# Attention on one core: both 64 by 64 corners side by side ahead of the value product, and the stores of x and of squared keys issued by GpSimd

## The chip, the core and the metric

The kernel runs on one core of one Trainium2 chip. The core has TensorE (PE, matmuls), VectorE (DVE), ScalarE (ACT), GpSimd (POOL) and SyncE (SP); each runs its own instructions in the order in which they were issued, and they wait for one another by semaphores. DMAs are issued from the engines' queues: in the kernel before nearly all by SyncE. The metric is the device time of one execution in microseconds (us), as the median of several runs. Less is better.

## What is computed

Four batches of 448 tokens, 12 heads of 64 columns (768 in all). Attention with a sigmoid in the place of the softmax, then a gated layer with squared keys, then a Fourier mix, a normalisation and two more matmuls:

```python
scores = scale * np.matmul(q, k.transpose(0, 1, 3, 2)) - np.log(S)
attn = 1.0 / (1.0 + np.exp(-scores))
x = np.matmul(attn, v)                      # heads side by side: B, S, 768
xk = mu_k * x + (1.0 - mu_k) * x_prev       # x_prev: one token earlier
xr = mu_r * x + (1.0 - mu_r) * x_prev
k = np.maximum(xk @ w_k, 0.0)
v = k * k @ w_v
y = v / (1.0 + np.exp(-(xr @ w_r)))
mixed = np.real(np.fft.fft(np.fft.fft(y, axis=1), axis=2))
u = y + mixed
un = (u - mean(u)) / np.sqrt(var(u) + 1e-06)
out = u + np.maximum(un @ w_ch1, 0.0) @ w_ch2
```

All in float32. Where it pays, the kernel splits a matrix into a high and a low part (names with `h` and `l`) and takes three matmuls of the fast kind instead of one in full float32.

## The kernel before

The program is written by a planner. Its class `Order` keeps a planned time of its own; generators for heads, keys, loads and weights are woken at due times and issue instructions when they are woken, with modelled costs. What comes out is one fixed order of instructions on each engine; on the chip nothing is reordered, only waited for.

The change lies in the attention stage, roughly the first 220 us. Two heads of one batch share 128 partitions and are a pair of columns; there are 24 such head pairs, `pairs`, numbered `i` from 0 to 23, six to a batch, and called heads below. The loop in `attention` takes two of them at a time. The 448 tokens of a head are three blocks of 128 and a rest of 64, the corner. For heads i and i + 1, from i = 6 on, a period goes like this:

- `begin(i - 2)` and `attnv` (twice): the value product of the two heads before. `begin` multiplies the two corners of the sigmoid (`sg_c`) with 64 rows of `v`, in 64x64 tiles of the array; `attnv` adds the six full blocks of each head (`sg`), in 128x64 tiles. Both sum into PSUM tiles `av`.
- `both(i)`: first `corner(i)`, the 64x64 scores of both heads (`sc_c`) in full float32 from raw `q` and `k`, then `scores(i)`, six score tiles `sc` of head i in 64x128 tiles, a stretch of key matmuls, `scores(i + 1)`, and a longer stretch of key matmuls.
- After each score tile ScalarE makes its sigmoid (`weigh`).
- `join` copies a finished `av` out of PSUM into `x` (ScalarE), stores `x` in DRAM, mixes it with the row of tokens before (`mix_k`) and splits it into `xkh` and `xkl`.
- `keys` multiplies them with the key weights, 18 matmuls for a tile `k`. The matmuls wait in a list (`feed`) and are issued one by one between the other steps. `key_done` takes a finished tile: ReLU out of PSUM and square (both `kt`), a cast to the high half of `kp` (ScalarE), the low half (VectorE), and the store of both halves, 448 KB, in DRAM. Its name there is `k2_d`; the views print `k_d<-kp`.

Buffers set what waits. Scores, corners, and the products `av` of heads 6 and on share six PSUM slots (`ps2`) in turn; key tiles have banks of their own (`bank`). `kp`, `kt` and `x` have two buffers each, so the cast into the third `kp` waits until the store of the first has landed, and `x` is overwritten when its store has landed. The raw `q` and `k` of two heads are loaded (960 KB in all) when `corner` of the two before has read theirs; `divide` then makes their halves `qh`, `ql`, `kh`, `kl`. In the gaps VectorE also splits weights (`wr_raw` to `wrh`, `wrl`, and `first_raw` to `first`); GpSimd clears a column of each `x` and stores the split `first` weights in DRAM, and does no more.

Heads 2 and 4 (`TURNS`) are an earlier form of the loop, in which the second `attnv` runs inside `both`.

Of the kernel before, what the change touches and what calls it, by code (L numbers as in the profile page):

```python
# [12 lines left out]
F32 = mybir.dt.float32  # L13
# [25 lines left out]
TURNS = (2, 4)  # L39
# [241 lines left out]
def build(tc, ap):  # L281
    nc = tc.nc
    V, G = nc.vector, nc.gpsimd
    o = Order(nc)
# [70 lines left out]
    x_d = [[dram.tile([128, S + 1], F32, name=f"x_d{b}_{p}") for p in range(NP)] for b in range(B)]  # L355
    k2_d = [[dram.tile([128, 2, S], F32, name=f"k2_d{b}_{f}") for f in range(NF)] for b in range(B)]
# [36 lines left out]
    pairs = [(b, p) for b in range(B) for p in range(NP)]  # L393
# [54 lines left out]
    def weigh(i, n, ps):  # L448
        sg = att.tile([128, S], F32, tag="sg", name=f"sg_{i}_{n}", bufs=2 * len(places) + 3)
        o.at["sg", i, n] = o.act(sg, ps[:, 0:S], AF.Sigmoid, bias=bias_s, scale=1.0 / math.sqrt(DH))  # L450
        sg_t[i, n] = sg

    def slot(name):
        return ps2.tile([128, 512], F32, tag="sc", name=name)
# [3 lines left out]
    def scores(i):  # L458
        k, q = pair_t["k", i], pair_t["q", i]
        for c in range(3):  # L460
            ps = [slot(f"sc_{i}_{2 * c + j}") for j in range(2)]
            if i < WHOLE:
                for j in range(2):
                    o.mm(ps[j][:, 0:S], k[half[j], c], q[half[j]], True, True, 0.39)
            else:
                for t, (a, b) in enumerate(TERMS):
                    for j in range(2):
                        o.mm(ps[j][:, 0:S], k[a][half[j], c], q[b][half[j]], t == 0, t == 2, 0.107)
            if c == 0:
                yield from o.others()  # L470
            for j in range(2):
                weigh(i, 2 * c + j, ps[j])
            yield from o.others()

    def corner(i):
        yield from o.need(*(("raw", w, i + m) for m in range(2) for w in "kq"))
        ps = [slot(f"sc_{i}_c{j}") for j in range(2)]
        for j in range(2):
            for m in range(2):
                k, q = raw_t["k", i + m], raw_t["q", i + m]  # L480
                o.mm(ps[j][half[m], 0:S], k[half[j], 3, 64 * j : 64 * j + 64], q[half[j]], True, True, 0.21)
        o.at["corner", i] = o.now
        yield from o.others()
        for j in range(2):
            weigh(i, f"c{j}", ps[j])
        yield from o.others()

    def soon(*keys):
        o.quiet = all(k in o.at for k in keys)

    def both(i, t0, turn=None):
        if i > 0:
            yield from corner(i)
        yield from o.need(("k", i), ("q", i))
        yield from scores(i)
        if i == 0:
            yield from corner(i)
        o.at["pair", i] = o.now
        o.quiet = o.quiet and i < WHOLE
        if turn:  # L500
            yield from turn
        if i >= WHOLE:
            yield t0 + (PACES[0] - AHEAD) * (len(o.feed) > 0)
            soon(("k", i + 1), ("q", i + 1))
            yield t0 + PACES[0] * (len(o.feed) > 0)
        yield from o.need(("k", i + 1), ("q", i + 1))
        yield from scores(i + 1)
        o.at["pair", i + 1] = o.now
        o.quiet = False

    def begin(i):
        ps = [(bank if i < WHOLE else slot)(f"av_{i + m}") for m in range(2)]
        yield from o.need(("sg", i, "c0"), ("sg", i, "c1"))
        for m in range(2):
            v = pair_t["v", i + m]
            for j in range(2):
                o.mm(ps[m][half[j], 0:S], v[half[m], 3, j], sg_t[i, f"c{j}"][half[m]], True, False, 0.21, skip=True)
        yield from o.others()
        av_t[i], av_t[i + 1] = ps

    def attnv(i):
        v = pair_t["v", i]
        for n, (c, j) in enumerate(places):
            yield from o.need(("sg", i, n))
            sg = sg_t.pop((i, n))
            o.mm(av_t[i][half[j], 0:S], v[:, c, j], sg, False, c == 2, 0.39, skip=True)
            if i % 2 and n == 2 and i < len(pairs) - 2 and i + 1 not in TURNS:
                g = i + 1
                soon(*(("raw", w, g + m) for w in "kq" for m in range(2)), ("k", g), ("q", g))
            yield from o.others()  # L530
        o.at["av", i] = o.now
        o.spawn(join(i, av_t.pop(i)), o.now + 0.2)
        yield from o.others()

    def join(i, ps):
        if i > 1:
            yield from o.issued(("mixed", i - 2))
        x = att.tile([128, S + 1], F32, tag="x", name=f"x_{i}")
        G.memset(x[:, 0:1], 0.0)
        yield o.act(x[:, 1 : S + 1], ps[:, 0:S])  # L540
        b, p = pairs[i]
        o.dma(x_d[b][p], x)
        if b > 1:
            yield from o.issued(("key", b - 2))
        xh = mop.tile([128, S], F32R, tag=f"xkh{p}", name=f"xkh_{i}")
        xl = mop.tile([128, S], F32R, tag=f"xkl{p}", name=f"xkl_{i}")
        xk_t[b, p] = (xh, xl)
        yield from mix(x, mu_k, att, p, f"k{i}", xh, xl, ("xk", b, p))
        o.at["mixed", i] = o.now

    def mix(x, mu, pl, p, nm, xh, xl, key, bufs=2):
        xk = pl.tile([128, S], F32, tag="mix", name=f"mix_{nm}", bufs=bufs)
        early = nm[0] == "k" and int(nm[1:]) < WHOLE
        if early:
            yield o.ts(xk, x[:, 1 : S + 1], mu[:, 0, p : p + 1], None, ALU.mult, ALU.bypass)
        else:
            yield from o.calm()
            yield o.act(xk, x[:, 1 : S + 1], AF.Copy, scale=mu[:, 0, p : p + 1])
        yield o.stt(xk, x[:, 0:S], mu[:, 1, p : p + 1], xk, ALU.mult, ALU.add)
        if early:  # L560
            V.tensor_copy(xh, xk)
            yield o.spend(V, 0.34)
        else:
            yield from o.calm()
            yield o.act(xh, xk)
        o.at[key] = t = o.sub(V, xl, xk, xh)
        yield t
# [6 lines left out]
    def attention():  # L574
        for i in range(0, len(pairs) + 2, 2):
            t0 = o.now
            turn = None
            if i > 0:
                yield from o.need(("v", i - 2), ("v", i - 1))
                yield from begin(i - 2)  # L580
                yield from attnv(i - 2)
                turn = attnv(i - 1)
                if i not in TURNS:
                    yield from turn
                    turn = None
            if i < len(pairs):
                yield from both(i, t0, turn)
            yield t0 + PACES[1] * (len(o.feed) > 0)
        yield from o.need(("xk", B - 1, NP - 1))
        o.at["attention"] = o.now  # L590

    def key_done(b, f, ps):
        t = mop.tile([128, S], F32, tag="kt", name=f"kt_{b}_{f}")
        o.act(t, ps, AF.Relu)
        yield from o.calm()
        yield o.act(t, t, AF.Square)
        parts = mop.tile([128, 2, S], F32R, tag="kp", name=f"kp_{b}_{f}")
        yield from o.calm()
        yield o.act(parts[:, 0], t)
        yield o.sub(V, parts[:, 1], t, parts[:, 0])  # L600
        o.at["k2_d", b, f] = o.dma(k2_d[b][f], parts.bitcast(F32)) + 2.0
        yield o.now

    def keys():
        for b in range(B):
            yield from o.issued(("av", NP * b + NP - 1))
            for f in range(NF):
                yield from o.need(("wk", f))

                def pair(t, b=b, f=f):  # L610
                    return wkh[:, f, t], wkl[:, f, t], *xk_t[b, t]

                ks = {p: ("xk", b, p) for p in range(NP)}
                yield from o.tile(partial(bank, f"k_{b}_{f}"), KD, pair, partial(key_done, b, f), None, ks)
                while len(o.feed) > 6:
                    yield o.now + 0.1
            while o.feed:
                yield o.now + 0.05
            o.at["key", b] = o.now
# [40 lines left out]
    for what in "kqv":  # L660
        o.spawn(prepare(what))
    o.spawn(attention())
    o.spawn(weights(), LATER)
    o.spawn(keys())
# [606 lines left out]
    for v, (g, ps) in enumerate(VISITS):  # L1271
        for j in range(2):
            i = 2 * (v - NG + PL) + j
# [469 lines left out]
```

## Time and profile before

| what | us |
|---|---|
| median of 3 runs | 1141.82 (1141.53 to 1143.3) |
| profiled execution, its own time | 1139.96 |
| span in the profile, first to last instruction | 1138.2 |
| TensorE busy | 1118.6 |
| VectorE busy | 810.6 |
| ScalarE busy | 649.2 |
| GpSimd busy | 16.1 |

The granted TensorE clock is 0.997 of full speed over the span. All rows come from the one profiled execution; its times are counted from the span's start. On the chain of work that ended last, 88% of the span is TensorE. Timelines show each instruction's start and length; instructions of an engine overlap a little, so the step from one to the next is read from their starts, or from a length less the overlap. One 64x64 matmul in the program is two rows on TensorE.

### The profile page before, as it was taken

Reading aid. Unit: us, or ns where it says so; the run is one execution under the profiler, and the core shown is the slowest. Engines: PE = TensorE matmul, PEld = TensorE weight load, DVE = VectorE, ACT = ScalarE, POOL = GpSimd, SP = SyncE. Lnnn points to the kernel's source line nnn. Section 1 sums busy time; section 2 is a strip of 40 time slices with the busy share of each in tenths; the row PEclk is TensorE's granted clock in tenths of the full one; section 3 lists DMA queues with packets and bytes.
Section 4 is the critical chain, followed back from the end, with each engine's and each line's share of the span. In section 5 each row is a group of like instructions: output and inputs, shape, how many; then the busy total and the mean of one; then the engine's idle time right before and its main releaser. Section 6 shows DMA issues by size and latency. Waiting matters only on the chain.

```text
span 1138.2 us, 16784 instructions
## 1 busy us (share of the span) xinstructions
PE 1118.6 (98%) x5908; PEld 975.0 (86%) x5908; DVE 810.6 (71%) x1306; ACT 649.2 (57%) x1165; POOL 16.1 (1%) x49
## 2 busy tenths in 40 slices
PE   9999999999999999989999999989999999999998
PEld 3476676799999989979999999879999999999997
DVE  3876767566624678799896565677657679976887
ACT  6788877766632333334686666667755444554442
POOL 0000001100000000000000000000000000000000
PEclk9999999999999999999999999999999999999999
DMA  7765789667939786536967988999887448945432
GB/s 247 237 231 202 241 325 342 256 231 262 335 136 313 278 305 226 179 134 227 298 230 249 301 300 276 319 318 360 271 332 267 135 151 283 360 145 184 160 99 86
DMA packets 116309, 279.65 MB, mean 246 GB/s; under 512 B 13248, under 2 KB 58496, under 8 KB 116096
## 3 DMA queue, kind: packets, MB, share of 16 engines
q1 hardware_dynamic: 113472, 266.29, 68.4%
q0 software_dynamic: 2464, 11.83, 2.8%
q8 instruction: 46, 0.75, 0.3%
q10 hardware_dynamic: 288, 0.46, 0.1%
q14 instruction: 39, 0.32, 0.1%
HBM read 184.80 MB, written 93.73 MB: 245 GB/s over the span
## 4 chain that ended last, share of the span: by engine, by line
PE 88%; DVE 5%; DMA 4%; ACT 2%; issue 1%; SPq 0%; DVEq 0%; ACTq 0%
PE m L213 23%; PE k L213 9%; PE f_Y L213 9%; PE v L213 8%; PE r L213 8%; PE av L213 6%; PE f_X L213 6%; PE f_W L213 6%; PE sc L213 5%; PE f L213 4%; PE pq L213 1%; PE sc_c L213 1%; DVE out L248 1%; PE pa L213 1%; PE qa L213 1%
## 5 line engine op out<-in xcount | busy, mean ns | idle before, releaser
L213 PE MATMUL m<-hs,sw 128*128 128x448 f32 x1512 | 303.7, 362 | 0.9 <-DVE hs L248 0.8
L213 PEld LDWEIGHTS m<-hs,sw 128*128 128x128 f32 x1512 | 283.3, 188 | 21.1 <-DVE hs L248 2.0
L265 ACT CAST sw<-w 128x768 fp32r<-128x768 f32 x84 | 70.0, 833 | 90.7 <-PE m L213 50.3
L265 ACT CAST hs<-r 128x896 fp32r<-128x896 f32 x84 | 78.9, 940 | 65.3 <-DVE r L248 65.3
L248 DVE TENSOR_TENSOR sw<-w,sw 128x768 fp32r<-128x768 f32 x84 | 80.2, 955 | 49.2 <-ACT sw L265 49.0
L213 PE MATMUL v<-k,wvh 128*128 128x448 f32 x384 | 111.5, 365 | 0.0
L248 DVE TENSOR_TENSOR hs<-r,hs 128x896 fp32r<-128x896 f32 x84 | 91.3, 1087 | 5.9 <-ACT hs L265 5.9
L267 ACT ACTIVATE sg<-sc,bias_s 128x448 f32<-128x448 f32 x144 | 78.3, 649 | 12.5 <-PE sc L213 12.4
L213 PE MATMUL f_Y<-T,blk 128*128 128x448 f32 x360 | 78.8, 367 | 4.3 <-ACT u L265 3.5
L213 PE MATMUL f_W<-T,blk 128*128 128x448 f32 x360 | 77.9, 364 | 0.4 <-DVE blk L248 0.4
L213 PEld LDWEIGHTS f_Y<-T,blk 128*128 128x128 f32 x360 | 68.1, 190 | 10.0 <-ACT u L265 4.2
L213 PEld LDWEIGHTS v<-k,wvh 128*128 128x128 f32 x384 | 71.9, 188 | 4.8 <-issue 0.4
L213 PEld LDWEIGHTS f_W<-T,blk 128*128 128x128 f32 x360 | 67.9, 189 | 5.4 <-DVE blk L248 0.8
L213 PE MATMUL k<-xkh,wkh 128*128 128x448 f32 x192 | 70.7, 368 | 0.9 <-ACT kt L267 0.9
L213 PE MATMUL k<-xkl,wkh 128*128 128x448 f32 x192 | 70.3, 366 | 0.0
L213 PE MATMUL v<-k,wvl 128*128 128x448 f32 x192 | 70.0, 365 | 0.0
L213 PE MATMUL k<-xkh,wkl 128*128 128x448 f32 x192 | 70.0, 364 | 0.0
L213 PE MATMUL f<-un,w1h 128*128 128x448 f32 x192 | 57.1, 374 | 4.5 <-DVE un L248 2.7
L267 ACT ACTIVATE w_raw<-w_raw 128x384 f32<-128x384 f32 x80 | 44.3, 553 | 23.9 <-DMA w_raw<-in_w 23.9
L213 PE MATMUL av<-sg,v 128*64 128x448 f32 x288 | 57.2, 544 | 0.0
L265 ACT CAST blk<-a 128x384 fp32r<-128x384 f32 x80 | 40.4, 513 | 28.3 <-PE f_Y L213 7.8
L256 DVE SCALAR_TENSOR_TENSOR w<-w_raw,w 128x384 uint32<-128x384 uint32 x60 | 33.3, 555 | 28.6 <-ACT w L267 24.6
(200 smaller groups left out, 2071.1 us busy)
## 6 DMA issues: line engine op xcount, KB each, us to landing
w<-v_d SPq DMA_DIRECT2D x84, 384.0 KB, 3.2
w_raw<-in_w SPq DMA_DIRECT2D x80, 384.0 KB, 4.6
r<-h_d SPq DMA_DIRECT2D x48, 448.0 KB, 5.8
k_d<-kp SPq DMA_DIRECT2D x32, 448.0 KB, 3.9
k<-k_d SPq DMA_DIRECT2D x32, 448.0 KB, 6.1
h_d<-h SPq DMA_DIRECT2D x56, 224.0 KB, 4.2
a<-w_d SPq DMA_DIRECT2D x32, 384.0 KB, 5.0
v_d<-w SPq DMA_DIRECT2D x48, 192.0 KB, 4.7
```

The lines of the kernel that those rows point to most:

```text
L213: self.nc.tensor.matmul(out, lhs, rhs, start=start, stop=stop, skip_group_check=skip)
L248: eng.tensor_tensor(out, a, c, op=op)
L256: self.nc.vector.scalar_tensor_tensor(out, a, scalar, c, op0=op0, op1=op1)
L265: self.nc.scalar.copy(out, a)
L267: self.nc.scalar.activation(out, a, fn, **kw)
```

## The change

`corner(i)` is called from `attention` ahead of `begin(i - 2)` for i = 6, 8, ... 22, and from `both` only for heads 2 and 4 (and 0, as before). The store of `x` (24 of 224.5 KB) and that of the squared keys (32 of 448 KB) get GpSimd as their engine (`G`).

```diff
     def both(i, t0, turn=None):
-        if i > 0:
+        if i in TURNS:
             yield from corner(i)
...
         yield o.act(x[:, 1 : S + 1], ps[:, 0:S])
         b, p = pairs[i]
-        o.dma(x_d[b][p], x)
+        o.dma(x_d[b][p], x, G)
...
             if i > 0:
+                if i < len(pairs) and i not in TURNS:
+                    yield from corner(i)
                 yield from o.need(("v", i - 2), ("v", i - 1))
                 yield from begin(i - 2)
                 yield from attnv(i - 2)
...
         yield o.sub(V, parts[:, 1], t, parts[:, 0])
-        o.at["k2_d", b, f] = o.dma(k2_d[b][f], parts.bitcast(F32)) + 2.0
+        o.at["k2_d", b, f] = o.dma(k2_d[b][f], parts.bitcast(F32), G) + 2.0
```

What a due time moves, the planner moves with it. Three places show it, all around heads 12 to 15; names carry running numbers, which differ between the two kernels. (In `kp_6` the 6 is the key tile within its batch.)

ScalarE from the high half of `kp_6` to the first sigmoid of head 14, before (`x` of heads 12 and 13, `sg_c` and `sg` of head 14):

```order
L265 CAST kp_6_1494<-kt_6_1428 128x448
L267 ACTIVATE kt_7_1505<-k_7_1426 128x448
L267 ACTIVATE kt_7_1505<-kt_7_1505 128x448
L265 CAST kh_1527<-k_1355 128x512
L265 CAST qh_1534<-q_1357 128x448
L265 CAST kp_7_1540<-kt_7_1505 128x448
L265 COPY x_1550<-av_1521 128x448
L265 COPY x_1582<-av_1522 128x448
L267 ACTIVATE sg_c_1585<-sc_c_1570,bias_s 128x448
L267 ACTIVATE sg_c_1587<-sc_c_1571,bias_s 128x448
L267 ACTIVATE sg_0_1602<-sc_0_1589,bias_s 128x448
```

and now:

```order
L265 CAST kp_5_1465<-kt_5_1407 128x448
L267 ACTIVATE kt_7_1512<-k_7_1434 128x448
L267 ACTIVATE kt_7_1512<-kt_7_1512 128x448
L265 CAST kp_6_1516<-kt_6_1437 128x448
L267 ACTIVATE sg_c_1542<-sc_c_1528,bias_s 128x448
L267 ACTIVATE sg_c_1544<-sc_c_1529,bias_s 128x448
L265 CAST kp_7_1559<-kt_7_1512 128x448
L265 COPY x_1570<-av_1546 128x448
L265 COPY x_1600<-av_1547 128x448
L267 ACTIVATE sg_0_1603<-sc_0_1589,bias_s 128x448
```

The corners' sigmoids come ahead of `kp_7` and of the two copies `x<-av` instead of behind them; the halves of `q` and `k` that stood here come earlier, ahead of `kp_5`.

VectorE from the low half of `kp_5` on, before (`wr_bits`, `wrh` and `wrl` are the split of a receptance weight):

```order
L248 TENSOR_TENSOR kp_5_1441<-kt_5_1397,kp_5_1441 128x448
L248 TENSOR_TENSOR xkl_1322<-mix_k_1323,xkh_1321 128x448
L256 SCALAR_TENSOR_TENSOR wr_bits<-wr_raw,wr_bits 128x768
L248 TENSOR_TENSOR kl_1476<-k_1336,kh_1475 128x512
L248 TENSOR_TENSOR ql_1481<-q_1338,qh_1480 128x448
L248 TENSOR_TENSOR kp_6_1494<-kt_6_1428,kp_6_1494 128x448
L256 SCALAR_TENSOR_TENSOR wr_bits<-wr_raw,wr_bits 128x768
L248 TENSOR_TENSOR kl_1528<-k_1355,kh_1527 128x512
L248 TENSOR_TENSOR ql_1535<-q_1357,qh_1534 128x448
L248 TENSOR_TENSOR kp_7_1540<-kt_7_1505,kp_7_1540 128x448
L344 CAST wrh_294<-wr_bits 128x768
L248 TENSOR_TENSOR wrl_295<-wr_bits,wrh_294 128x768
```

and now, from that weight's first bits:

```order
L256 SCALAR_TENSOR_TENSOR wr_bits<-wr_raw,wr_bits 128x768
L248 TENSOR_TENSOR ql_1481<-q_1314,qh_1480 128x448
L256 SCALAR_TENSOR_TENSOR wr_bits<-wr_raw,wr_bits 128x768
L248 TENSOR_TENSOR kl_1484<-k_1316,kh_1483 128x512
L248 TENSOR_TENSOR xkl_1389<-mix_k_1390,xkh_1388 128x448
L248 TENSOR_TENSOR xkl_1341<-mix_k_1342,xkh_1340 128x448
L344 CAST wrh_294<-wr_bits 128x768
L248 TENSOR_TENSOR wrl_295<-wr_bits,wrh_294 128x768
L248 TENSOR_TENSOR kp_5_1465<-kt_5_1407,kp_5_1465 128x448
L248 TENSOR_TENSOR kp_6_1516<-kt_6_1437,kp_6_1516 128x448
L248 TENSOR_TENSOR kp_7_1559<-kt_7_1512,kp_7_1559 128x448
```

All three `kp` now stand behind `wrh` and `wrl`; `kp_5` had been ahead of both steps on `wr_bits`.

TensorE from the last two value products of head 13 on, before:

```order
L213 MATMUL av_1522<-sg_4_1466,v_1311 64x448
L213 MATMUL av_1522<-sg_5_1468,v_1311 64x448
L213 MATMUL sc_c_1570<-q_1338,k_1336 64x448
L213 MATMUL sc_c_1570<-q_1357,k_1355 64x448
L213 MATMUL sc_c_1571<-q_1338,k_1336 64x448
L213 MATMUL sc_c_1571<-q_1357,k_1355 64x448
L213 MATMUL sc_0_1589<-qh_1480,kh_1475 128x448
```

and now, from the last key matmul ahead of the product:

```order
L213 MATMUL k_0_1510<-xkh_1111,wkl 128x448
L213 MATMUL sc_c_1528<-q_1299,k_1301 64x448
L213 MATMUL sc_c_1528<-q_1314,k_1316 64x448
L213 MATMUL sc_c_1529<-q_1299,k_1301 64x448
L213 MATMUL sc_c_1529<-q_1314,k_1316 64x448
L213 MATMUL av_1546<-sg_c_1304,v_1128 64x448
L213 MATMUL av_1546<-sg_c_1306,v_1128 64x448
L213 MATMUL av_1547<-sg_c_1304,v_1332 64x448
L213 MATMUL av_1547<-sg_c_1306,v_1332 64x448
L213 MATMUL av_1546<-sg_0_1359,v_1128 64x448
```

The four `sc_c` have moved from behind the 16 matmuls of the product to its start, directly ahead of the four `av<-sg_c`. The same holds for the other eight pairs; nothing else moves on TensorE.

On GpSimd the stores stand in one queue with the cleared columns: here first the column of `x` of head 12, then the stores of `kp_5`, of that `x`, of `kp_6` and of `kp_7`, the column of the next `x` and its store.

## Rows read from the trace of the kernel before

**Rows 1.** The page, its part 1: busy us (share) and instructions of each engine.

```profile
PE 1118.6 (98%) x5908; PEld 975.0 (86%) x5908; DVE 810.6 (71%) x1306; ACT 649.2 (57%) x1165; POOL 16.1 (1%) x49
```

**Rows 2.** Table by stretches: us, then busy us (instructions) by engine, clock, DMA share, GB/s.

```profile
100.00:160.00 60.00, 59.85 (x362) 40.38 (x361) 43.55 (x68) 47.89 (x93) 3.55 (x10) 1.00 0.72 257
```

**Rows 3.** Waits, 0 to 262: engine, line, waited for: us in total, times, longest us.

```profile
PE k L213 <- ACT kt L267: 0.9, 3, 0.5
PE warm L657 <- DVE bias_s L387: 0.9, 1, 0.9
...
ACT kp L265 <- DMA k_d<-kp: 3.1, 4, 1.3
```

**Rows 4.** Timeline of TensorE: start us, us, engine, line, op, out<-in, shape, count.

```profile
89.01 0.98 PE L213 MATMUL av<-sg_c,v 64*64 64x448 f32 x8
89.92 4.73 PE L213 MATMUL av<-sg,v 128*64 128x448 f32 x24
94.59 0.98 PE L213 MATMUL sc_c<-q,k 64*64 64x448 f32 x8
95.50 0.47 PE L213 MATMUL sc<-qh,kh 64*128 64x448 f32 x2
95.81 0.37 PE L213 MATMUL sc<-ql,kh 64*128 64x448 f32 x2
96.01 0.37 PE L213 MATMUL sc<-qh,kl 64*128 64x448 f32 x2
...
97.22 0.49 PE L213 MATMUL sc<-qh,kl 64*128 64x448 f32 x2
97.64 0.47 PE L213 MATMUL k<-xkl,wkh 128*128 128x448 f32 x1
```

**Rows 5.** Timeline of TensorE, a period and two periods later: the last two score tiles.

```profile
117.28 0.50 PE L213 MATMUL sc<-qh,kh 64*128 64x448 f32 x2
...
138.17 0.49 PE L213 MATMUL sc<-qh,kh 64*128 64x448 f32 x2
```

**Rows 6.** Timeline of ScalarE, heads 12 to 15; in brackets idle time ahead and its releaser.

```profile
106.75 0.59 ACT L265 CAST xkh<-mix_k 128x448 fp32r<-128x448 f32 x1
...
108.14 0.66 ACT L265 CAST kh<-k 128x512 fp32r<-128x512 f32 x1
108.67 0.59 ACT L265 CAST qh<-q 128x448 fp32r<-128x448 f32 x1
...
111.99 0.57 ACT L265 CAST kp<-kt 128x448 fp32r<-128x448 f32 x1 [0.23 <-DMA k_d<-kp]
112.96 0.53 ACT L265 COPY x<-av 128x448 f32<-128x448 f32 x1 [0.40 <-PE av L213]
...
126.75 0.60 ACT L265 CAST xkh<-mix_k 128x448 fp32r<-128x448 f32 x1
```

**Rows 7.** Timeline of VectorE in the same stretch.

```profile
109.88 0.95 DVE L256 SCALAR_TENSOR_TENSOR wr_bits<-wr_raw,wr_bits 128x768 uint32<-128x768 uint32 x1
110.75 0.69 DVE L248 TENSOR_TENSOR kl<-k,kh 128x512 fp32r<-128x512 f32 x1
...
114.43 0.62 DVE L248 TENSOR_TENSOR kp<-kt,kp 128x448 fp32r<-128x448 f32 x1
114.97 0.55 DVE L344 CAST wrh<-wr_bits 128x768 fp32r<-128x768 f32 x1
115.55 0.96 DVE L248 TENSOR_TENSOR wrl<-wr_bits,wrh 128x768 fp32r<-128x768 f32 x1
```

**Rows 8.** Stores: `k_d<-kp` by SyncE, 112 to 119; `w_d<-first_bits` by GpSimd, 138 to 206, 206 to 222.

```profile
DMA to landing us min/median/max: 4.1/5.8/7.5
...
L274 POOL DMA_DIRECT2D w_d<-first_bits x6: 544/547/829, 139.0 to 197.8; - x6
DMA to landing us min/median/max: 4.6/6.0/8.2
...
DMA to landing us min/median/max: 3.0/3.1/3.2
```

## The prediction

> **What bounds the kernel now.** I read the page first: TensorE is busy nearly all of the span, GpSimd 16 us of it [rows 1]. Then the table by stretches: of the 60 us from 100 to 160, in the attention stage, TensorE is busy 59.85, VectorE and ScalarE about 44 and 48 [rows 2]. So a gain must be time that TensorE loses between matmuls, and a loss appears as soon as one of the two vector engines hands something over late. The waits of the first 262 us say who could: TensorE waited 0.9 us for a `kt` and otherwise only at the warm-up; ScalarE waited 3.1 us in four places, 1.3 at most, for the store of an earlier `kp` to land [rows 3]. The rows of TensorE around one product of heads [rows 4] and of ScalarE and VectorE beside the next one [rows 6, 7] give the prices.
>
> Beyond the attention stage the order of instructions on every engine is the same in both kernels, except that the last stores of squared keys leave from GpSimd. I take nothing there.
>
> **The corners side by side.** In the kernel before, the 64x64 scores `sc_c` and the 64x64 products `av<-sg_c`, 0.91 us each (89.01 to 89.92, 94.59 to 95.50), are apart, so the array changes shape four times in a period; side by side it changes three times. The price of one change: the eight `sc_c` take 0.91 us; their four pairs at the steady step of 0.20 (95.81 to 96.01) would take 0.80, so 0.11 is lost on entry. The next shape's first step is 0.31 (95.50 to 95.81), 0.11 over the steady step again [rows 4]. Whether a removed change gives back one or both isn't shown: 0.11 to 0.21, taken in the middle, 0.16. Nine pairs are moved: 9 x 0.16 = **1.4 us** (1.0 to 1.9).
>
> The second gain: the step out of the first head's scores is 0.42 (97.22 to 97.64), where the bare change of shape costs 0.31 [rows 4]. The last two score tiles wait there for PSUM that `sg_c` frees. With `sg_c` done during the product that wait goes: 0.11 in each of eight periods (the ninth, at head 8, waits for other tiles), **0.9 us** (0 to 0.9). What is late next in that place is `x`: in the changed kernel the same two score tiles wait for the copies of both `x` out of PSUM.
>
> **The order on ScalarE.** Casts of the next heads' `q` and `k` now stand ahead of the `kt` that frees a bank for TensorE, two of them at heads 12 and 13, one at 18. They cost 0.46 and 0.53 (rows of 0.59 and 0.66 that overlap the next by 0.13) [rows 6]: at most 0.99 + 0.46 = 1.45. Before, TensorE already had to wait for `kt` in three places [rows 3], so little slack can absorb it, while the `sg_c` moved ahead give some back: I take **1.1 us** (0 to 1.5) of loss.
>
> **The stores of squared keys.** `kp` has two buffers, so the cast of `kp_7` needs the store of `kp_5` landed. Before, ScalarE waited 0.23 us for exactly this at 111.99 and then copied `x` at 112.96 [rows 6]. Three edits meet here. VectorE now makes the low half of `kp_5` behind the split of a receptance weight; the store is GpSimd's; and the loads of the next heads start some 5.5 us earlier (the length of the product, 89.01 to 94.59 [rows 4]), since the corner that frees their buffers is ahead of the product, and so lie beside the store. The chain, head 14: ScalarE is free at 106.75 and casts `qh_15` until 107.2 [rows 6]. From there VectorE has, back to back (rows overlap the next by 0.08): `ql` 0.54, the weight's bits 0.87, `kl` 0.61, two `xkl` of 0.54, `wrh` 0.58, `wrl` 0.88, `kp_5` 0.54, together 5.1 [rows 7]. The store goes out at 107.2 + 5.1 + 0.1 = 112.4. When it has landed, ScalarE casts `kp_7` (0.46, as `qh`, of the same shape) and copies both `x` (0.53 each), with 0.1 for hand-overs 1.6 us. TensorE wants those banks at 117.28 by the rows of before [rows 5], 117.1 with one change of shape less. With a landing of L the stall is 112.4 + L + 1.6 - 117.1 = **L - 3.1**.
>
> The same pattern stands at head 16 (`kp_2` of batch 1 behind `kp_0`): ScalarE free at 126.75 [rows 6], `qh_17` to 127.2, 5.1 of VectorE, store at 132.4, copies done at 134.0 + L, wanted at 138.17 - 0.16 = 138.0 [rows 5]: **L - 4.0**. At head 20 (`kp_7` behind `kp_5`) ScalarE waited before too, up to 1.3 [rows 3], without holding TensorE; the weight's split isn't ahead there, and I take 0 (up to 2). At head 10 `kp_0` goes out early enough by the same reckoning, and I take 0.
>
> How long is L? The trace has no store of 448 KB from GpSimd. The nearest rows are its stores of 384 KB: amid traffic 4.6 to 8.2, median 6.0; in quiet 3.0 to 3.2 [rows 8]. SyncE's own stores of 448 KB took 4.1 and 7.5 beside such loads [rows 8]. At 112 and 132 the loads are in flight, so I take 6.0, with 3.1 and 8.2 as ends. Then the stalls are 2.9 + 2.0 = **4.9 us** (0 at 3.1; 1.5 + 0.6 = 2.1 at 4.6; 5.1 + 4.2 = 9.3 at 8.2).
>
> The Trainium skill speaks for a shorter one: by "DMA: Bandwidth & Descriptors", section "Queues, rings and completion order", each DMA engine takes turns between the queues that have work, packet by packet, so a store on a queue of its own wouldn't stand behind the loads. By that rule L is near the quiet 3.1 and the stalls are nothing. The stores of 384 KB lie on the same separate queue and took 6.0 amid traffic [rows 8], so the trace doesn't bear it out.
>
> **The stores of x, and what leaves SyncE.** Twenty-four issues of 0.55 us on an engine with 16 us of work [rows 1, 8] cost nothing themselves. GpSimd works in order: behind the store of `x_12`, which waits for the held copy, stand the stores of `kp_6` and `kp_7`; the next casts that need them come some 8 us later, which covers a stall of the size above. On SyncE 56 issues less let loads start earlier. TensorE waits for no load in this stage [rows 3], so earlier loads buy nothing and only crowd the stores.
>
> **Sum** against the profiled execution of 1139.96: -1.4 - 0.9 + 1.1 + 4.9 = +3.7, so 1143.7. The median of the runs, 1141.82, lies 1.86 above that execution: **1145.5**.
>
> **Rivals.** The measurement can tell about 0.2%, 2.3 us, from no change.
>
> *The stores land in time (no change).* L of 3.1 to 5.2: the stalls are at most 2.1 + 1.2 = 3.3, the sum -1.2 to +2.1, median 1140.6 to 1143.9; at 4.6, the fastest of the crowded rows, +0.9 and 1142.7. For it: two of six crowded rows. Against it: those stores are smaller.
>
> *The gains stand alone (faster).* It decides at two points: both stores land within 3.1 us, and the casts moved ahead of `kt` fall into ScalarE's idle time. A change of shape then gives back 0.21: -1.9 - 0.9 = -2.8, and 1139.0. For it: ScalarE is idle 12 of 60 us [rows 2] and waits before each `x` copy. Against it: the two places where the casts moved are those where TensorE has no reserve.
>
> *The slow end (slower).* GpSimd's descriptors wait while VectorE holds it up, in the stage in which VectorE is most loaded. Then both stores take the longest row, 8.2 [rows 8]: -1.2 + 9.3 = +8.1, 1149.9. In the rows the issue itself took 0.54 to 0.83 us [rows 8], so a hold of 0.3 is seen at the most.
>
> The Trainium skill states this rule on "SBUF — State Buffer", section "SBUF: two separate sides": VectorE in its two-port modes locks GpSimd out of their shared port, and a DMA issued from GpSimd took some 3.1 us instead of 0.62 beside a VectorE copy. By it each of the two stores would be about 2.5 us later, an estimate from that page, and the sum +8.7. The short issue rows speak against so much.
>
> **How the numbers follow.** My forecast, landing above 5.3 us at both places, 0.49, and the slow end 0.06: slower 0.55. In time 0.33, all within 0.2%. The gains alone 0.12. For the range: the case in time reaches down to 1140.6, a part of the faster one lies just below it, and the slow end gives 1149.9; with 1140.2 to 1149.5 about 2 in 10 are left out, most of the faster case and the slow end. The likeliest case's own range is 1144.1 (L of 5.3) to 1149.5.
>
> **What would show it.** Right: ScalarE's waits for the landing of `k_d<-kp` grow from 3.1 us to over 8, most of it near heads 14 and 16, and TensorE's `sc` wait there for the copies of `x` by 2 to 3 us each; `sc_c` and `av<-sg_c` together take 1.66 rather than twice 0.91; the step out of the first head's scores falls from 0.42 to 0.31. Wrong: stores of `kp` landing in under 4.6 us, or `kp_5` made by VectorE before 111, which takes the stall away; `sc_c` and `av<-sg_c` still 1.82 together, which takes the first gain away; waits for `kt` that stay at 0.9, so that the casts cost nothing; or a wait for a load on TensorE, which no step here has.

## The result and the profile after

| | before | after |
|---|---|---|
| median, us | 1141.67 (4 runs) | 1153.62 (4 runs) |
| ratio | | 1.0119 (95% interval 1.0100 to 1.0139) |
| profiled execution, us | 1139.96 | 1154.46 |
| span, us | 1138.2 | 1152.5 |

The change costs 12 us. I had forecast the direction and the mechanism, but a third of the size: 1145.5 where 1153.6 was measured, with 1149.5 as the upper end of the range.

The loss lies in the attention stage. The last key matmul of the stage is followed by the first receptance matmul `r`, here in the kernel before and then after (timeline of TensorE: start us, length us, engine, line, operation, out<-in, shape, count):

```profile
256.38 0.36 PE L213 MATMUL r<-xrh,wrh 128*128 128x448 f32 x1
```

```profile
267.67 0.36 PE L213 MATMUL r<-xrh,wrh 128*128 128x448 f32 x1
```

So 11.3 of the 14.3 us between the spans are gone by 268 us; another 2.7 come in the value stage, where TensorE's order is the same (below). The waits of the first 275 us after the change answer [rows 3] (engine, line, waited for: us in total, times, longest):

```profile
PE sc L213 <- ACT x L265: 6.4, 3, 4.6
PE k L213 <- ACT kt L267: 1.9, 4, 0.9
...
ACT kp L265 <- DMA k_d<-kp: 12.2, 6, 4.4
```

TensorE now waits for `x`, 6.4 us in three places, and ScalarE 12.2 us for the landing of `kp` stores, where it had been 3.1. The first of the three places is head 14. TensorE there (in brackets idle time ahead and its releaser), against [rows 4, 5]:

```profile
109.98 0.98 PE L213 MATMUL sc_c<-q,k 64*64 64x448 f32 x8
...
111.64 4.73 PE L213 MATMUL av<-sg,v 128*64 128x448 f32 x24
116.30 0.48 PE L213 MATMUL sc<-qh,kh 64*128 64x448 f32 x2
...
122.65 1.17 PE L213 MATMUL sc<-qh,kh 64*128 64x448 f32 x2 [4.56 <-ACT x L265]
...
124.50 0.74 PE L213 MATMUL k<-xkh,wkh 128*128 128x448 f32 x1
...
125.41 0.57 PE L213 MATMUL k<-xkh,wkl 128*128 128x448 f32 x1
125.78 0.57 PE L213 MATMUL k<-xkh,wkh 128*128 128x448 f32 x1
...
126.49 0.37 PE L213 MATMUL k<-xkh,wkl 128*128 128x448 f32 x1
...
129.99 0.47 PE L213 MATMUL sc<-qh,kh 64*128 64x448 f32 x2
```

The corners side by side take 1.66 us (109.98 to 111.64) instead of twice 0.91: the gain is there. Then the last two score tiles wait 4.6 us for the copies of `x`, and what follows is slow: the step from one key matmul to the next is 0.37 us until 126.49, nearly twice the 0.20 of before. The granted clock says why (table by stretches; busy us and instructions of PE, PEld, DVE, ACT and POOL, then the clock as a share of 2.4 GHz, DMA share, GB/s):

```profile
120.00:125.00 5.00, 2.35 (x7) 1.61 (x8) 2.70 (x5) 3.40 (x8) 1.88 (x3) 0.50 0.42 167
125.00:130.00 5.00, 5.00 (x24) 4.32 (x22) 4.93 (x8) 4.30 (x9) 0.71 (x3) 0.86 0.95 316
...
190.00:195.00 5.00, 5.00 (x19) 4.22 (x19) 0.20 (x1) 5.00 (x10) 2.70 (x6) 0.66 0.99 391
```

In the stall the clock falls to 0.50, that is 1.2 GHz, and it is given back only after some 4 us of renewed work (122.65 to 126.49). After the third wait, at head 20, the clock is low again (190 to 195). TensorE there:

```profile
189.55 0.90 PE L213 MATMUL sc<-qh,kh 64*128 64x448 f32 x2 [1.67 <-ACT x L265]
...
190.79 0.48 PE L213 MATMUL k<-xkh,wkh 128*128 128x448 f32 x1
...
197.00 0.47 PE L213 MATMUL sc<-qh,kh 64*128 64x448 f32 x2
```

The scores that began at 186.40 last 4.4 us instead of 2.15, the key matmuls behind them 6.2 instead of 4.61.

ScalarE at head 14, against [rows 6]:

```profile
107.25 0.60 ACT L265 CAST qh<-q 128x448 fp32r<-128x448 f32 x1
...
109.16 0.60 ACT L265 CAST kp<-kt 128x448 fp32r<-128x448 f32 x1
...
121.60 0.56 ACT L265 CAST kp<-kt 128x448 fp32r<-128x448 f32 x1 [4.43 <-DMA k_d<-kp]
122.07 0.96 ACT L265 COPY x<-av 128x448 f32<-128x448 f32 x2
```

and VectorE, against [rows 7]:

```profile
107.19 0.56 DVE L260 TENSOR_SCALAR wr_raw<-wr_raw 128x768 f32<-128x768 f32 x1
...
109.25 0.62 DVE L248 TENSOR_TENSOR ql<-q,qh 128x448 fp32r<-128x448 f32 x1
...
113.79 0.62 DVE L248 TENSOR_TENSOR kp<-kt,kp 128x448 fp32r<-128x448 f32 x1
```

and the store from GpSimd, with its landing:

```profile
114.71 0.54 POOL L274 DMA_DIRECT2D k_d<-kp  x1 [10.48 <-DVE kp L248]
```

```profile
DMA to landing us min/median/max: 6.8/6.8/6.8
```

The chain of the prediction is seen link by link: `qh_15`, VectorE's work, `kp_5` at 113.79, the store at 114.71, landed at 121.5, `kp_7` at 121.60, both `x`, then TensorE.

### The profile page after: what moved, and what is told of

Read it like the earlier page. It is cut to its first block, busy times and chain, and to the rows that moved or that the text cites. A ratio compares the mean times of both kernels' runs of the same rounds, so it can differ in the third digit from the quotient of the medians.

```text
span 1152.5 us, 16802 instructions
## 1 busy us (share of the span) xinstructions
PE 1125.0 (98%) x5908; PEld 978.9 (85%) x5908; DVE 811.1 (70%) x1306; ACT 650.0 (56%) x1165; POOL 47.1 (4%) x105
## 4 chain that ended last, share of the span: by engine, by line
PE 74%; DVE 6%; DMA 6%; ACT 2%; issue 1%; SPq 0%; ACTq 0%; DVEq 0%
PE m L213 23%; PE v L213 8%; PE f_Y L213 8%; PE r L213 7%; PE k L213 7%; PE f_W L213 5%; PE f_X L213 5%; PE f L213 4%; PE av L213 1%; PE sc L213 1%; PE pq L213 1%; DMA k_d<-kp 1%; DVE out L248 1%; PE pa L213 1%; PE qa L213 1%
## 5 line engine op out<-in xcount | busy, mean ns | idle before, releaser
L267 ACT ACTIVATE sg<-sc,bias_s 128x448 f32<-128x448 f32 x144 | 78.4, 646 | 14.3 <-PE sc L213 14.2
L248 DVE TENSOR_TENSOR blk<-a,blk 128x384 fp32r<-128x384 f32 x80 | 43.8, 554 | 14.7 <-ACT blk L265 14.6
```

The source lines that it names most:

```text
L248: eng.tensor_tensor(out, a, c, op=op)
L267: self.nc.scalar.activation(out, a, fn, **kw)
```

## The experiments

The question was which part of this is the cause: the corners' place, the casts that it lets go ahead, GpSimd's queue, or the landing as such. Each group of experiments had its own chip, and its medians are set against runs of the kernel before on the same chip: 1140.8 for the corners alone, both kinds of store, the three casts behind `x` and the repeated matmuls; 1141.2 for the stores of squared keys alone, the casts put back for heads 14 and 15, and the stores of `x` on GpSimd with those of squared keys on SyncE; 1142.1 for the rest.

**Which half of the change.** First the corners alone:

```diff
-        o.dma(x_d[b][p], x, G)
+        o.dma(x_d[b][p], x)
...
-        o.at["k2_d", b, f] = o.dma(k2_d[b][f], parts.bitcast(F32), G) + 2.0
+        o.at["k2_d", b, f] = o.dma(k2_d[b][f], parts.bitcast(F32)) + 2.0
```

> The corners moved as in the change, all stores issued by SyncE as before; the order on TensorE, ScalarE and VectorE is that of the changed kernel. My theory (the corner's move reorders ScalarE and VectorE so that a cast of squared keys stands ahead of the copies of x and waits for a store that leaves late; who issues the store matters little): the store of kp_5 leaves at about 114.8 behind the loads and lands 4 to 7.5 us later, TensorE waits for x 2 to 5 us at head 14, median 1149 to 1155. Rival (GpSimd's queue is what makes the store late): the store lands within 3 us, median 1141 to 1143.

Measured: 1157.85, ratio 1.0155 (1.0126 to 1.0184); the interval overlaps that of the full change (1.0100 to 1.0139). Waits of TensorE, then the store on SyncE, its landing, and ScalarE behind it:

```profile
PE sc L213 <- ACT x L265: 9.8, 3, 6.5
```

```profile
116.19 0.42 SPq L274 DMA_DIRECT2D k_d<-kp  x1
```

```profile
DMA to landing us min/median/max: 8.2/8.2/8.2
```

```profile
124.46 0.56 ACT L265 CAST kp<-kt 128x448 fp32r<-128x448 f32 x1 [6.49 <-DMA k_d<-kp]
```

So the corners' move makes the loss by itself. In the profile TensorE's waits for `x` are even longer than after the full change, 9.8 us instead of 6.4: SyncE issues the store 1.5 us later (the period itself is 1.2 later), behind the loads, and it lands in 8.2 us instead of 6.8. Whether GpSimd's queue makes the loss smaller in the median is not shown. The cause is as in my theory, but the time lies above its range.

Then the stores alone, the corners where they were:

> The corners where they were before, both kinds of store issued by GpSimd; the order on TensorE, ScalarE and VectorE is that of the kernel before. My theory: kp_5 is made by 109.4 and lands by 115.5 at the latest, TensorE waits under 1 us for x, median 1141 to 1144. Rival (GpSimd's queue is the cause): most of the 12 us, 1148 or more.

```diff
-        o.dma(x_d[b][p], x)
+        o.dma(x_d[b][p], x, G)
...
-        o.at["k2_d", b, f] = o.dma(k2_d[b][f], parts.bitcast(F32)) + 2.0
+        o.at["k2_d", b, f] = o.dma(k2_d[b][f], parts.bitcast(F32), G) + 2.0
```

Measured: 1146.56, ratio 1.0041 (1.0019 to 1.0063): between the two expectations, and TensorE does not wait for `x` at all. The profile shows a stall that I had not named. On GpSimd the store of a weight's bits is issued behind four stores of `kp` and `x`, and lands 8.3 us later; VectorE stands still for it, with `mix_k` queued behind:

```profile
159.39 0.54 POOL L274 DMA_DIRECT2D w_d<-first_bits  x1
```

```profile
DMA to landing us min/median/max: 8.3/8.3/8.3
```

```profile
167.74 0.56 DVE L260 TENSOR_SCALAR first_bits<-first_raw 128x768 uint32<-128x768 uint32 x1 [8.47 <-DMA w_d<-first_bits]
...
170.21 0.68 DVE L256 SCALAR_TENSOR_TENSOR mix_k<-x,mu_k,mix_k 128x448 f32<-128x448 f32 x1
```

```profile
172.91 0.47 PE L213 MATMUL k<-xkh,wkh 128*128 128x448 f32 x1 [2.51 <-ACT kt L267]
```

`mix_k` comes 6.7 us later than in the kernel before (163.47 there), ScalarE's `xkh` waits for it with the next `kt` behind, and TensorE waits 2.5 us for that `kt`. Behind this wait, too, the granted clock falls: 0.75 from 175 to 180.

**Either kind of store alone.** To see which stores do this, the kernel before with one kind on GpSimd:

```diff
-        o.dma(x_d[b][p], x)
+        o.dma(x_d[b][p], x, G)
```

> The kernel before with the stores of x alone issued by GpSimd. stores_only lost about 4 us at head 18, where the store of a weight's bits landed 8.3 us after its issue behind stores of x and kp in GpSimd's queue and VectorE stood still for it. Theory (either kind of store in that queue is enough, in proportion to its bytes): 1141.5 to 1144. Rival (only the kp stores matter): 1140 to 1141.5, no more waiting for the weight store than before (8.7 us).

```diff
-        o.at["k2_d", b, f] = o.dma(k2_d[b][f], parts.bitcast(F32)) + 2.0
+        o.at["k2_d", b, f] = o.dma(k2_d[b][f], parts.bitcast(F32), G) + 2.0
```

> The kernel before with the stores of squared keys alone issued by GpSimd. Stores of x alone cost nothing (1140.3), both kinds 4.7 us. Theory (448 KB each in the queue of the weight stores are enough to hold those back until VectorE's split of the next weight stands still at head 18): wait for w_d<-first_bits over 12 us, TensorE waits over 2 us for a kt near 170, 1143 to 1147. Rival (only both kinds together fill the queue): 1139.5 to 1142, no such wait.

Measured: stores of `x` alone 1140.26, ratio 0.9986 (0.9973 to 0.9999); stores of squared keys alone 1142.17, ratio 1.0005 (0.9995 to 1.0015). VectorE's wait for the weight stores is longer in both than the 8.7 us of before, but its longest piece is 6.3 and 4.7 us, not 8.5, and TensorE's waits for `kt` are the 0.9 us of before:

```profile
DVE first_bits L260 <- DMA w_d<-first_bits: 16.7, 4, 6.3
```

```profile
DVE first_bits L260 <- DMA w_d<-first_bits: 13.1, 5, 4.7
```

(first with the stores of `x`, then with those of `kp`). So neither kind costs a measurable time alone; only both together delay the weight store far enough. Both my theories, that one kind is enough, fell.

**The stalls themselves.** If the loss is a cast that stands at the head of ScalarE's line, three casts moved behind the copies of `x` must give it back:

```diff
+LATE = {(0, 7): 13, (1, 2): 15, (1, 7): 19}
...
         yield o.act(x[:, 1 : S + 1], ps[:, 0:S])
+        o.at["x", i] = o.now
...
+        if (b, f) in LATE:
+            yield from o.issued(("x", LATE[b, f]))
         yield from o.calm()
         yield o.act(parts[:, 0], t)
```

> The changed kernel with three casts of squared keys (kp_7 and kp_2 of the first two batches and kp_7 of the second: those that waited at heads 14, 16 and 20) issued behind the copies of x instead of ahead of them; TensorE's order is unchanged. Theory (the stalls are these casts' wait at the head of ScalarE's line): TensorE's wait for x falls from 6.4 us to under 0.5, clock 1.00 throughout, median 1141 to 1143. Rival (the landing of stores or the port holds other things up as well): 1146 or more.

Measured: 1143.40, ratio 1.0028 (1.0017 to 1.0040): 2.6 us above its own runs of the kernel before, where the full change is 12 above. Waits of TensorE:

```profile
PE k L214 <- ACT kt L268: 2.2, 4, 1.0
...
PE sc L214 <- ACT x L266: 0.5, 1, 0.5
```

The waits for `x` are down to 0.5. It is 0.4 us above what I expected; the waits for `kt` remain, which this edit doesn't touch.

**Why the store leaves late.** The next kernel leaves the `kp` casts ahead of `x` and GpSimd its stores, and only puts the casts of the next heads' `q` and `k` back behind the first `kp` of their period:

```diff
+AFTER = {14: (0, 5), 16: (1, 0), 20: (1, 5)}
...
+        if i // 2 * 2 in AFTER:
+            yield from o.issued(("kp", *AFTER[i // 2 * 2]))
         yield from o.calm()
         if i == WHOLE:
...
+        o.at["kp", b, f] = o.now
         yield o.act(parts[:, 0], t)
```

> The changed kernel, but the halves of q and k of heads 14 to 17, 20 and 21 are cast behind the first kp of their period again, as in the kernel before; the kp casts still stand ahead of the copies of x and all stores are GpSimd's; TensorE's order is that of the changed kernel. Theory (the store of kp_5 is late because the earlier loads let these casts, and VectorE's work behind them, go ahead of kp): the store leaves near 110 instead of 114.7, lands by 116, TensorE's waits for x fall from 6.4 us to under 1, the first wait for kt at 98 goes, median 1141 to 1144. Rival (a store from GpSimd lands too late wherever it leaves): waits for x over 3 us, 1148 or more.

Measured: 1140.22, ratio 0.9985 (0.9968 to 1.0001). The store, its landing, and the cast of `kp_7` on ScalarE:

```profile
110.01 0.54 POOL L276 DMA_DIRECT2D k_d<-kp  x1 [13.31 <-DVE kp L250]
```

```profile
DMA to landing us min/median/max: 3.0/3.0/3.0
```

```profile
113.12 0.56 ACT L267 CAST kp<-kt 128x448 fp32r<-128x448 f32 x1
```

The store leaves 4.7 us earlier, ahead of the burst of loads, and lands in 3.0 instead of 6.8; `kp_7` no longer waits, and the wait for `x` is gone from TensorE's list. VectorE's order goes back with ScalarE's: it makes the low half of `kp_5` at 109.10 instead of 113.79, ahead of the weight's `wrh` and `wrl`. This settles it: the cause is the order of a few casts and of VectorE's work behind them. That the earlier loads let them go ahead is read from the program, in which these casts come due when their load has landed; after the change those loads leave 5.5 us earlier (90.16 instead of 95.67). Its runs spread from 1138.0 to 1143.1; the profiled one, 1143.04, has the stall at head 18 of the stores-only kernel (TensorE waits 3.2 us for a `kt`).

The same edit for heads 14 and 15 alone asks whether time gained at one stall is lost at the next:

```diff
-AFTER = {14: (0, 5), 16: (1, 0), 20: (1, 5)}
+AFTER = {14: (0, 5)}
```

> The changed kernel with the casts of q and k put back behind kp for heads 14 and 15 alone. Theory (each stall is its own, and the granted clock that falls behind it belongs to it): the stall at head 14 with its slow clock (6.0 and 0.9 us over the period before the change) and the wait for kt at 97 (0.7) go, the stalls at heads 16 and 20 stay, so 7.6 us of the 12: median 1145 to 1147.5. Rival (time gained at head 14 is lost again at the next two): 1149 or more.

Measured: 1145.73, ratio 1.0040 (1.0025 to 1.0055): 4.6 us above its own runs of before, so 7.4 of the 12 come back, near the 7.6 reckoned, and the stalls at heads 16 and 20 stay (`PE sc` waits for `x` 2.6 us in two places). That the sum fits is in part luck: at head 20 the wait grew from 1.7 to 2.3 us, but the clock did not fall behind it.

**The clock.** To separate the slow clock from the stall, matmuls of the score tiles were repeated where TensorE had stood still:

```diff
+                for _ in range({14: 7, 20: 3}.get(i, 0) if c == 1 else 0):
+                    for t, (a, b) in enumerate(TERMS):
+                        for j in range(2):
+                            nc.tensor.matmul(ps[j][:, 0:S], k[a][half[j], c], q[b][half[j]], start=t == 0, stop=t == 2)
```

> The changed kernel with the score matmuls of blocks 2 and 3 of heads 14 and 20 repeated 7 and 3 times (4.3 and 1.9 us of TensorE work ahead of the two stalls; same result, same order elsewhere), so that TensorE computes where it stood still. Theory (part of the loss is the granted clock that falls after the stall, about 4 us in the profile): the stall at head 14 is replaced by work, the clock stays at 1.00, median 1149 to 1150.5. Rival (the clock has nothing to do with the stalls): unchanged, 1153 to 1154.

Measured: 1154.24, ratio 1.0119 (1.0102 to 1.0136), no faster than the full change, so by the median my expectation fell. The profile says that the clock did as expected:

```profile
120.00:125.00 5.00, 5.00 (x43) 3.88 (x40) 1.95 (x4) 2.62 (x6) 1.09 (x2) 1.00 0.41 164
...
190.00:195.00 5.00, 5.00 (x27) 4.38 (x27) 0.06 (x1) 5.00 (x11) 2.59 (x6) 1.00 0.97 363
```

It stays at 1.00, and the stage ends 1.7 us earlier than after the change (265.96 against 267.67), but what follows takes nearly as much longer. There the granted clock falls in another place, and for longer than after the change (see the value stage below). So these profiles show that the clock is low after these two stalls and isn't when work takes their place; what that is worth in the median is not shown.

**Both orders put right.** The edits with `AFTER` and with `LATE` together, with three assignments of the stores:

> As casts_back, and the three kp casts behind the copies of x as in x_first. Theory: no wait for x, kt waits as before the change, and the two gains on TensorE (0.16 and 0.13 us a period, 2.4 us) are left, less what the weight stores lose behind the stores of x and kp in GpSimd's queue (0 to 2 us): median 1139.5 to 1142. Rival (something else in the change costs time): 1143 or more, as x_first.

> As both_orders, with all stores of x and squared keys on SyncE as before the change. Theory (once no kp cast stands ahead of x, the late landing of a store is covered, and GpSimd's queue has the weight stores to itself): 1138.5 to 1141, no worse than both_orders. Rival (SyncE's stores behind waiting loads are what GpSimd cures): slower than both_orders by 2 us or more.

> The corners moved, both orders put right (casts and copies of x as in both_orders), stores of x by GpSimd, of squared keys by SyncE. Theory (only the squared keys' stores harm GpSimd's queue): 1138.5 to 1140.5, no slower than both_orders_sp (1139.5), and no stall at head 18 in the profile. Rival: over 1141.5.

| stores of x, of squared keys | median | ratio to before |
|---|---|---|
| GpSimd, GpSimd | 1140.42 | 0.9986 (0.9973 to 1.0000) |
| SyncE, SyncE | 1139.45 | 0.9977 (0.9962 to 0.9992) |
| GpSimd, SyncE | 1139.62 | 0.9988 (0.9975 to 1.0002) |

Waits of TensorE in the second of them, and the first `r`:

```profile
PE sc_c L215 <- DMA q<-in_q: 0.5, 1, 0.5
PE k L215 <- ACT kt L269: 0.5, 2, 0.3
```

```profile
255.00 0.36 PE L215 MATMUL r<-xrh,wrh 128*128 128x448 f32 x1
```

All three medians lie where they were expected. With all stores on SyncE the kernel is 0.2% faster than the kernel before, and in the profile the attention stage ends 1.4 us earlier (255.00 against 256.38). The three are not to be told apart from each other, and 0.2% is at the edge of what these runs can tell: the stores of `x` alone came out at 0.9986 with nothing gained in the stage. In this form the move of the corners is a small gain on TensorE in the profile, and the move of the stores is no gain that can be measured.

## Why the prediction was right and wrong

*Corners side by side, -1.4.* Right in size for seven of the nine pairs, from head 10 on: 1.66 us instead of 1.82, 1.1 us together. At heads 6 and 8 nothing is gained: the two groups take 2.6 and 2.1 us instead of 1.8 and 1.9. At head 6 TensorE's weight load for the corner also waits 0.8 us for `k<-in_k`, a wait for a load, which the prediction had excluded.

*The step out of the first head's scores, -0.9.* Right at five of the eight heads, 0.7 us: the scores of head 12 take 2.01 us instead of 2.15. At the other three (14, 16, 20) the stalls stand in its place.

*Casts ahead of `kt`, +1.1.* Right: the key matmuls behind the scores of head 12 (97.41 to 102.76) take 5.35 us instead of 4.61, those of the longer stretch at head 18 (173.64 to 180.07) 6.43 instead of 5.97, 1.2 us together.

*The stall at head 14, +2.9.* The place, the chain and the formula were right; the size was not, for two reasons. The scores and the keys behind them took 8.19 and 5.49 us (116.30 to 124.50 to 129.99) instead of 2.15 and 4.61, 6.9 more. First, I let VectorE's chain begin with `ql_15` as soon as ScalarE had cast `qh_15`. But VectorE was still at the weight's first steps, which stand ahead of `ql_15` in its order (107.19 to 109.25 above), and ScalarE was 0.5 us later than reckoned, behind the wait for `kt` of my own third term. From `ql` to `kp` the chain took 5.2 us, as reckoned (5.1), but it began 2.0 late, so the store left at 114.7 and not at 112.4. The landing was 6.8, 0.8 more than the 6.0 that I took. Second, there is no term for the clock: about 2 us of the 6.9 are matmuls at 1.2 GHz behind the stall (122.65 to 126.49). The prediction treated a stall as a pure delay.

*The stall at head 16, +2.0.* 0.7 more than before: the store landed in 4.4 us, not in 6.0, and L - 4.0 is then 0.4.

*Head 20, taken at 0.* This is the step that failed outright: 2.2 us at the scores and 1.6 in the slow key matmuls behind. I had looked for a receptance weight's split ahead of `kp_5` there. What stands ahead of its low half on VectorE are halves of the next `q` and `k` and the first steps of another weight (`first_bits`), and these wait 1.7 us for the landing of an earlier `first_bits` store in GpSimd's queue:

```profile
179.97 0.56 DVE L260 TENSOR_SCALAR first_bits<-first_raw 128x768 uint32<-128x768 uint32 x1 [1.69 <-DMA w_d<-first_bits]
...
182.99 0.62 DVE L248 TENSOR_TENSOR kp<-kt,kp 128x448 fp32r<-128x448 f32 x1
```

The stall doesn't need this wait: with the corners moved and all stores of `x` and `kp` on SyncE it is 0.55 us, and the scores of head 20 take 5.1. With the casts put back the stall is gone. Head 20 and the clock at head 14 together are 5.8 us that the sum left out; heads 14, 16 and 20 cost 11.4 us where it had 4.9.

*Stores of `x` and `kp` in GpSimd's queue.* I reckoned their issues and what stands behind them among themselves, and left out the stores that were there already. VectorE's wait for `w_d<-first_bits` grew from 8.7 to 21.3 us. With the corners where they were, the two kinds of store cost 0.4%; in the full change they hold VectorE up at head 20, above, and what that costs is not shown.

*The rivals.* The slow end, 1149.9, came nearest, but by a mechanism that the trace doesn't show: GpSimd held up by VectorE. After the change the 32 stores of `kp` took GpSimd 0.54 us to issue in the median and 0.90 at the most, against 0.54 to 0.83 for the weight stores before [rows 8], and the store that left at 110 with the casts put back landed in 3.0 us. The row (ns, least, median, most):

```profile
L274 POOL DMA_DIRECT2D k_d<-kp x32: 539/539/897, 66.7 to 270.6; - x32
```

By the Trainium skill, "SBUF — State Buffer", section "SBUF: two separate sides", a DMA from GpSimd beside a VectorE copy takes some 3.1 us where it takes 0.62 alone; no run here shows an issue as long as that.

The rule of the Trainium skill on turns between queues ("DMA: Bandwidth & Descriptors", section "Queues, rings and completion order") says that each DMA engine serves them in turn, packet by packet. It fits in direction: from the queue of its own the store landed in 6.8 us, behind SyncE's loads in 8.2, though the two left at different moments of the loads. A landing as short as in quiet the trace doesn't show.

*After 268 us.* I took nothing beyond the attention stage, and that failed too: the value stage, from the first `v` to the first `f`, takes 152.3 us instead of 149.6, with the same order on TensorE. The granted clock tells for the most part why. In both kernels TensorE waits 2.2 to 2.4 us there for `sq`, but behind this wait the clock falls in the profile of after and not in that of before. The stretches (us, PE busy, clock, DMA share, GB/s) of before, of after, and of the kernel with repeated matmuls:

```profile
425.00:430.00 5.00, 5.00 (x44) 1.00 0.54 163
```

```profile
435.00:440.00 5.00, 3.77 (x13) 0.70 0.81 253
```

```profile
435.00:440.00 5.00, 5.00 (x20) 0.50 0.61 203
```

From the end of the wait to the same later matmul it is 5.35 us (435.69 to 441.04) after the change and 3.75 before (423.28 to 427.03): 1.6 of the 2.7. All profiles fit: in the five without the fall (before, the stores together and either kind alone, both orders put right with all stores on GpSimd) the value stage takes 149.4 to 149.6 us, in the other eight 150.8 to 153.5, most with the repeated matmuls. Why the clock falls there in some and not in others is not shown.

## What to carry to other kernels

Where a planner orders instructions, an edit that lets a load start earlier also lets everything behind that load go ahead of other work: read on each engine what has been overtaken, and for every step of a chain ask not only what it waits for but when its engine comes free. A wait that reaches TensorE costs more than its length where the granted clock falls in it or behind it, and that can happen in a stage that the change doesn't touch. And before stores are sent to a quieter queue, list the stores that are in it and who waits for those.

## What was not expected of the hardware

In and behind a wait of 4.6 us the granted clock was 0.50, and the step from one key matmul to the next was 0.37 us until 3.8 us after the wait. A wait of 1.7 us at head 20 was followed by 0.66 in the next 5 us; but when the same place waited 2.3 us in the kernel with heads 14 and 15 put back, the clock stayed at 1.00:

```profile
180.00:185.00 5.00, 2.74 (x15) 2.05 (x14) 1.16 (x3) 3.76 (x8) 2.24 (x6) 1.00 0.94 370
185.00:190.00 5.00, 5.00 (x35) 4.27 (x33) 2.84 (x4) 4.89 (x10) 0.53 (x2) 1.00 0.93 362
```

So the length of a single wait doesn't tell whether the clock falls, and the wait for `sq` in the value stage says the same. A store of 448 KB landed in 3.0 us when it left just ahead of the loads, in 6.8 beside them from another queue, and in 8.2 behind them in the same one.
